# Turning k and q of chunks 2 and 3 on TensorE instead of VectorE and DMA, in a kernel of gated linear attention and a SoLU feed-forward block

## The chip, the core and the metric

The kernel runs on one core of one Trainium2 chip. The core has TensorE (PE in the profile; its weight loads are PEld), VectorE (DVE), ScalarE (ACT), GpSimd (POOL) and SyncE (SP, which here only issues DMAs). Each engine executes its own list of instructions in order and waits on semaphores for the others. The metric is the device time of one execution in microseconds (us); lower is better.

## The reference

Two blocks follow each other. The first is a recurrence over 768 time steps for 4 batches and 8 heads with head dimension 48; the second works on the 3072 resulting rows of 384.

```python
mag = np.sqrt(a_re * a_re + a_im * a_im)
scale = np.minimum(mag, 0.999) / (mag + 1e-06)
a_re_n, a_im_n = (a_re * scale, a_im * scale)
for t in range(S):
    ...
    new_re = ar * S_re - ai * S_im
    new_im = ar * S_im + ai * S_re
    kv = np.einsum('bhd,bhe->bhde', k[:, :, t], v[:, :, t])
    S_re, S_im = (new_re + kv, new_im)
    y[:, :, t] = np.einsum('bhd,bhde->bhe', q[:, :, t], S_re)
...
h = x @ w_in
e = np.exp(h - h_max)
sm = e / (np.sum(e, axis=-1, keepdims=True) + 1e-09)
solu = h * sm
ln = (solu - mu) / np.sqrt(var + 1e-06) * g_ln
return (ln @ w_out).astype(np.float32)
```

The weights w_in (384 x 1024), w_out (1024 x 384) and g_ln come as float64 and are converted on the chip.

## The kernel before

**Tiling.** The 768 steps are cut into 6 stretches of 128, so there are 24 chunks (stretch times batch), numbered c = stretch * 4 + batch. Two chunks make a group g; the gates of a group are prepared together. So group 0 holds chunks 0 and 1, group 1 holds chunks 2 and 3.

**Preparing a group** (prep_steps, L793). From a_re and a_im the magnitudes and angles are formed by a chain that alternates between ScalarE and VectorE: `inverse` (Ln, Exp), `ratio` (two products on VectorE), `sure`, `tangent`, `square`, `secant`, `size`, `eps`, `lnm`. `total0/1` sums the logarithms over time on TensorE (f_L, L848), `grow` and `decay` are four Exp on ScalarE, `trig` loads the table for trigonometric functions, `angle` is an arctangent, `phase0/1` sums the angles on TensorE (f_phase, L848), `nearest` and `part` wrap them, `sin` and `cos` fill the tile f_cs, `exp` (a step of that name) loads the Exp table again. `qs` and `ks` scale q and k. In group 0 the first part runs in two halves, with a or b at the end of the step's name. The steps `last` and `onward` are small DMAs that hand the end of a stretch on.

**Turning k and q** (turn_steps, L949). `k2` and `q2` on VectorE (L957) multiply k and q by cosine and sine into f_kq, 128 x (2, 8, 96). For the scores it is needed with time in the free dimension (f_kqT). There are two ways. Chunks in the list `SHORT_KQ` (0 and 1) go through TensorE: `kt0, kt1, qt0, qt1` each transpose four heads into PSUM (f_turned, L978, four instructions), and `kT0, kT1, qT0, qT1` copy them on ScalarE (L984). The PSUM pool `ps_t` for this has two buffers, which f_L, f_phase, f_tot, f_zt, f_parts and f_count use too. All other chunks go through `kqb`, one transpose of 32 x 32 blocks on VectorE (f_kb, L966), and `kqt0`, four DMAs from SP that put the blocks in place (L971).

**A chunk** (chunk_steps, L998). `score0/1` (TensorE, L1011), `mask0` (VectorE, L1016), `values` (TensorE, L1044, result f_y), and, except in the last stretch, `carry` (TensorE, f_d, L1052) and `add` (VectorE, state).

**The feed-forward part of a chunk** (ffn_steps, L1073). `turned_x` copies f_y to f_xT on ScalarE (L1078); `up0/1` multiply by w_in (f_h, L1085); `exp0` is the exponential on ScalarE with its sum; `solu` the product on VectorE; then z is turned (`zt/zT` through TensorE and ScalarE for the chunks in `SHORT`, `blocks/away` through VectorE and DMA for the others); `down0/1` multiply by w_out (f_o, L1162); `centred`, `spread`, `norm`, `scale` normalise; `store` is the output DMA. In the trace TensorE's float32 matmuls stand as two records each.

**The weights** (weight_steps, L721). Seven pieces, 0 to 2 of w_in and 3 to 6 of w_out, are fetched as float64 into one of three buffers f_raw (`fetch`), and converted: `raised` on ScalarE (L746), `convert` on VectorE in three instructions (L752, L754, L756). `mean` 0 to 7, `meansum` and `centre` 0 to 7 subtract the mean from w_out. Near the end each piece is fetched again (`again`) and looked at for its least magnitude (`inspect`, L759); `judge`, `judges`, `judgew`, `count` and `flag` end in a flag that chooses between ending and a slower general program.

**What sets the order.** Everything is written out by hand: the string ORDER (L515 to L600) names every step with its index, and the loop at L1257 issues them in this order. The order of the instructions of one engine is the order in which the string names its steps; there is no scheduler. SP's list of DMAs follows the same string.

Of the kernel before, what the change touches and what calls it, by code (L numbers as in the profile page):

```python
# [515 lines left out]
load_ara:0 inversea:0 load_aia:0 ratioa:0 surea:0 load_arb:0 tangenta:0 inverseb:0 squarea:0 load_aib:0 secanta:0  # L516
fourtha:0 ratiob:0 sureb:0 sizea:0 fetch:5 epsa:0 tangentb:0 squareb:0 secantb:0 lnma:0 fetch:1 raised:5 load_k:0
sizeb:0 fetch:0 epsb:0 total0:0 convert:5 load_q:0 fourthb:0 raised:1 grow0:0 decay0:0 lnmb:0 total1:0 grow1:0 fetch:2
decay1:0 convert:1 trig:0 anglea:0 angleb:0 ks1:0 phase0:0 phase1:0 load_vr:0 raised:0 convert:0 nearest0:0 nearest1:0
load_ar:1 part0:0 cosa:0 sina:0 qs0:0 qs1:0 load_ai:1 part1:0 ks0:0 sinb:0 fetch:6 cosb:0 q2:0 last:0 exp:0 qt0:0  # L520
qT0:0 raised:2 k2:0 qt1:0 qT1:0 kt0:0 kt1:0 load_v:0 q2:1 convert:2 kT0:0 inverse:1 fetch:3 fetch:4 gain:0 kT1:0 qt1:1
raised:6 k2:1 score0:0 onward:0 kt0:1 qT1:1 score1:0 turn_ends:0 ratio:1 kT0:1 load_k:1 sure:1 mask0:0 tot:0 tangent:1
values:0 convert:6 square:1 turned_x:0 secant:1 fourth:1 qt0:1 raised:3 size:1 convert:3 eps:1 qT0:1 load_q:1 lnm:1
up1:0 up0:0 raised:4 exp0:0 convert:4 total1:1 total0:1 grow1:1 ks1:1 decay0:1 grow0:1 decay1:1 trig:1 kt1:1 load_ar:2
angle:1 carry:1 kT1:1 phase0:1 ks0:1 load_ai:2 qs0:1 last:1 nearest0:1 solu0:0 phase1:1 nearest1:1 part0:1 score1:1
part1:1 score0:1 sin:1 mask0:1 zt1:0 qs1:1 cos:1 add:1 mean:0 load_q:2 mean:1 exp:1 mean:3 zT1:0 q2:2 values:1 k2:2
mean:7 inverse:2 load_v:1 mean:5 mean:4 mean:2 turned_x:1 mean:6 turn_ends:1 kqb:2 ratio:2 meansum:0 carry:0 up0:1
kqt0:2 centre:6 zt0:0 tot:1 sure:2 centred:0 centre:5 tangent:2 centre:7 square:2 up1:1 score0:2 score1:2 secant:2
spread:0 centre:4 centre:1 centre:0 size:2 zT0:0 k2:3 eps:2 centre:2 centre:3 down0:0 load_vr:1 fourth:2 q2:3 lnm:2
total1:2 exp0:1 total0:2 kqb:3 decay0:2 grow1:2 load_k:3 grow0:2 mask0:2 add:0 decay1:2 trig:2 down1:0 load_k:2  # L530
solu0:1 angle:2 on:2 values:2 kqt0:3 onward:1 zt0:1 centred:1 qs0:2 turned_x:2 zT0:1 carry:2 phase1:2 phase0:2 last:2
load_ar:3 nearest0:2 norm:0 score0:3 score1:3 ks1:2 nearest1:2 part0:2 scale:0 part1:2 sin:2 add:2 up1:2 cos:2
load_ai:3 up0:2 mask0:3 ks0:2 exp:2 q2:4 k2:4 inverse:3 values:3 exp0:2 load_v:2 turn_ends:2 load_q:3 zt1:1 kqb:4
ratio:3 zT1:1 solu0:2 turned_x:3 sure:3 down0:1 centred:2 tangent:3 kqt0:4 down1:1 tot:2 spread:1 square:3 zt1:2
secant:3 zt0:2 qs1:2 size:3 up1:3 carry:3 zT0:2 q2:5 k2:5 load_vr:2 fourth:3 eps:3 up0:3 store:0 norm:1 scale:1
score1:4 lnm:3 zT1:2 kqb:5 total1:3 add:3 total0:3 onward:2 exp0:3 load_ar:4 score0:4 down0:2 decay0:3 decay1:3
grow1:3 mask0:4 grow0:3 load_k:4 solu0:3 kqt0:5 qs0:3 centred:3 down1:2 blocks:3 spread:2 trig:3 angle:3 values:4 on:3
turned_x:4 phase1:3 phase0:3 last:3 norm:2 ks0:3 nearest0:3 carry:4 nearest1:3 part0:3 load_v:3 score1:5 ks1:3 away:3
part1:3 score0:5 add:4 up1:4 sin:3 cos:3 scale:2 qs1:3 exp:3 store:1 load_ai:4 spread:3 load_q:4 up0:4 mask0:5
turn_ends:3 inverse:4 q2:6 values:5 k2:6 kqb:6 exp0:4 ratio:4 turned_x:5 solu0:4 sure:4 tangent:4 down0:3 norm:3  # L540
kqt0:6 down1:3 centred:4 square:4 blocks:4 carry:5 secant:4 size:4 up1:5 tot:3 store:2 k2:7 eps:4 q2:7 scale:3 up0:5
score1:6 lnm:4 score0:6 onward:3 kqb:7 exp0:5 away:4 total1:4 load_vr:3 fourth:4 load_ar:5 total0:4 down0:4 decay0:4
solu0:5 grow1:4 grow0:4 mask0:6 decay1:4 trig:4 kqt0:7 centred:5 qs0:4 angle:4 down1:4 blocks:5 add:5 spread:4 on:4
store:3 values:6 away:5 phase0:4 last:4 turned_x:6 phase1:4 norm:4 ks0:4 nearest0:4 carry:6 nearest1:4 part0:4 part1:4
add:6 score0:7 sin:4 score1:7 ks1:4 up1:6 scale:4 up0:6 mask0:7 qs1:4 load_ai:5 turn_ends:4 spread:5 load_q:5 down0:5
cos:4 q2:8 values:7 exp:4 k2:8 inverse:5 kqb:8 exp0:6 ratio:5 load_k:5 down1:5 turned_x:7 solu0:6 sure:5 tangent:5
kqt0:8 carry:7 square:5 blocks:6 secant:5 norm:5 away:6 load_vr:4 fourth:5 up0:7 size:5 up1:7 k2:9 eps:5 q2:9
centred:6 score0:8 tot:4 score1:8 lnm:5 total0:5 kqb:9 scale:5 total1:5 load_v:4 exp0:7 decay0:5 down0:6 grow1:5
grow0:5 mask0:8 decay1:5 solu0:7 kqt0:9 qs0:5 down1:6 add:7 centred:7 spread:6 values:8 blocks:7 trig:5 angle:5
onward:4 on:5 last:5 phase0:5 turned_x:8 norm:6 phase1:5 away:7 ks0:5 nearest0:5 carry:8 nearest1:5 up1:8 part1:5  # L550
part0:5 store:5 scale:6 add:8 score0:9 sin:5 cos:5 score1:9 ks1:5 qs1:5 load_ar:6 load_ai:6 spread:7 load_q:6 up0:8
# [59 lines left out]
def whole(ctx, tc, flag, q, k, v, a_re, a_im, moe_w_in, moe_w_out, moe_g_ln, out):  # L611
# [58 lines left out]
    least = const.tile([P, 7], FP, name="f_least")  # L670
    T, steps = {}, {}

    SHORT_KQ = [0, 1]

    SHORT = [0, 1, 2, 23]

# [642 lines left out]
```

## Time and profile before

| | us |
|---|---|
| median of 3 runs | 423.92 (423.43 to 425.55) |
| the profiled execution, its time | 421.44 |
| its span in the trace | 419.1 |
| DVE busy | 331.8 (79%) |
| ACT busy | 287.5 (69%) |
| DMA queue of SP, share of 16 engines' span | 72.3% |

The profile is of one execution. Its groups of instructions give a count and a mean duration; the costliest on TensorE:

```profile
L1085 PE MATMUL f_h<-f_w_in,f_xT 128*32 128x512 f32 x1152 | 130.7, 593 | 0.4 <-ACT f_xT L1078 0.4
L1162 PE MATMUL f_o<-f_w_out,f_zT 128*32 128x384 f32 (+1 forms) x1344 | 130.1, 486 | 0.3 <-ACT f_zT L1117 0.2
```

The columns are line, engine, operation, output <- inputs, partitions x elements, count | busy us, mean ns of one | idle us of the engine just before them and what ended it. Matmuls overlap, so busy time is less than count times mean. A row of 40 digits gives the busy share of each fortieth of the span (10.5 us) in tenths.

### The profile page before, as it was taken

What the parts mean: (1) busy time and instruction counts of PE and PEld (TensorE: products, weight loads), DVE (VectorE), ACT (ScalarE), POOL (GpSimd) and SP (SyncE); (2) the same over time, 40 slices, a digit from 0 to 9 for tenths busy, and PEclk for the clock granted to TensorE, in tenths of its full rate; (3) what the DMA queues carried; (4) which work ended last, traced back from release to release, by engine and by line L of the source; (5) the groups of instructions that cost most, each with busy time, mean ns of one, the idle gap of its engine ahead of it and who ended that gap; (6) DMA issues with size and microseconds to landing.
All of it is one profiled execution on the core that took longest, in us unless ns stands there. A gap on an engine that the chain in (4) does not pass through costs nothing.

```text
span 419.1 us, 15795 instructions
## 1 busy us (share of the span) xinstructions
PE 381.9 (91%) x6928; PEld 200.4 (48%) x6928; DVE 331.8 (79%) x429; ACT 287.5 (69%) x468; POOL 57.0 (14%) x139
## 2 busy tenths in 40 slices
PE   0258779999999999999999999999999999999993
PEld 0025344555554554554555555555455544545441
DVE  4899899788799689699699599689798798774550
ACT  5898978888577768677667767866866885621440
POOL 3000000321210201021211211102111111010210
PEclk9988999999999999999999999999999999999998
DMA  8999436875858738769589857788868869478970
GB/s 235 311 262 215 86 83 127 180 159 113 194 137 173 176 93 179 151 149 206 122 191 201 176 125 157 189 180 192 167 141 196 167 156 204 94 170 256 328 260 28
DMA packets 167261, 72.58 MB, mean 173 GB/s; under 512 B 142480, under 2 KB 155792, under 8 KB 166416
## 3 DMA queue, kind: packets, MB, share of 16 engines
q1 hardware_dynamic: 167040, 71.17, 72.3%
q8 instruction: 56, 0.92, 0.9%
q10 hardware_dynamic: 144, 0.33, 0.3%
q14 instruction: 21, 0.17, 0.1%
HBM read 38.87 MB, written 4.72 MB: 104 GB/s over the span
## 4 chain that ended last, share of the span: by engine, by line
PE 79%; ACT 9%; DMA 4%; DVE 3%; issue 2%; SPq 0%; POOL 0%; DVEq 0%; ACTq 0%; POOLq 0%
PE f_o L1162 28%; PE f_h L1085 26%; PE f_y L1044 9%; PE f_score L1011 5%; PE f_phase L848 4%; PE f_L L848 4%; PE f_d L1052 3%; DMA f_ar<-in_a_re_dram 2%; DMA f_raw<-in_moe_w_out_dram 1%; DMA f_kqT<-f_kb 1%; PE f_zt L1112 1%; ACT f_cs L912 1%; ACT L946 1%; DVE f_kb L966 1%; ACT f_cs L907 1%
## 5 line engine op out<-in xcount | busy, mean ns | idle before, releaser
L1085 PE MATMUL f_h<-f_w_in,f_xT 128*32 128x512 f32 x1152 | 130.7, 593 | 0.4 <-ACT f_xT L1078 0.4
L1162 PE MATMUL f_o<-f_w_out,f_zT 128*32 128x384 f32 (+1 forms) x1344 | 130.1, 486 | 0.3 <-ACT f_zT L1117 0.2
L1162 PEld LDWEIGHTS f_o<-f_w_out,f_zT 128*32 128x32 f32 (+1 forms) x1344 | 55.0, 114 | 64.9 <-issue 55.0
L1085 PEld LDWEIGHTS f_h<-f_w_in,f_xT 128*32 128x32 f32 x1152 | 39.7, 110 | 64.8 <-issue 64.0
L966 DVE STREAM_TRANSPOSE f_kb<-f_kq 128x1536 f32<-128x1536 f32 x22 | 56.0, 2544 | 2.6 <-DMA f_kqT<-f_kb 2.2
L1095 ACT ACTIVATE f_z<-f_h 128x1024 f32<-128x1024 f32 x24 | 28.6, 1193 | 15.5 <-PE f_h L1085 15.5
L1078 ACT COPY f_xT<-f_y 128x384 f32<-128x384 f32 x24 | 11.4, 474 | 39.8 <-PE f_y L1044 39.8
L1011 PEld LDWEIGHTS f_score<-f_kqT 96*32 96x32 f32 x1536 | 32.7, 111 | 10.4 <-issue 9.8
L1044 PE MATMUL f_y<-f_att,f_v 128*32 128x128 f32 (+1 forms) x384 | 36.1, 273 | 1.2 <-DVE f_att L1016 1.2
L1104 DVE SCALAR_TENSOR_TENSOR f_z<-f_h,f_z 128x1024 f32<-128x1024 f32 (+1 forms) x36 | 33.4, 962 | 3.9 <-ACT f_z L1095 3.9
L1044 PE MATMUL f_y<-f_att,f_vr 128*32 128x128 f32 x384 | 36.4, 273 | 0.0
L1140 POOL TENSOR_SCALAR f_less<-f_sum 128x1 f32<-128x1 f32 x24 | 13.1, 546 | 163.4 <-DVE f_z L1104 152.7
L1016 DVE TENSOR_TENSOR f_att<-f_score,f_mats 128x1024 f32<-128x1024 f32 x24 | 29.1, 1213 | 7.2 <-PE f_score L1011 7.2
L903 DVE SCALAR_TENSOR_TENSOR f_f<-f_f,f_phase 128x384 f32<-128x384 f32 x24 | 13.0, 552 | 26.8 <-ACT f_f L899 26.5
L848 PE MATMUL f_L<-f_lr,f_mats 128*32 128x384 f32 x192 | 19.3, 518 | 15.7 <-DVE f_lr L843 15.7
L1011 PE MATMUL f_score<-f_kqT 96*32 96x32 f32 (+3 forms) x1536 | 32.8, 236 | 0.0
L1044 PE MATMUL f_y<-f_kqT,f_state 96*32 96x128 f32 (+1 forms) x640 | 32.7, 272 | 0.0
L1143 ACT ACTIVATE f_z<-f_z,f_less 128x1024 f32<-128x1024 f32 x24 | 27.5, 1147 | 0.0
L1166 ACT ACTIVATE f_ot<-f_o,f_rs 128x384 f32<-128x384 f32 x24 | 13.7, 573 | 16.5 <-POOL f_rs L1151 6.0
L1044 PEld LDWEIGHTS f_y<-f_att,f_v 128*32 128x32 f32 (+1 forms) x384 | 21.8, 103 | 6.2 <-issue 3.8
L1122 DVE STREAM_TRANSPOSE f_zb<-f_z 128x1024 f32<-128x1024 f32 x20 | 24.8, 1238 | 0.1
L957 DVE TENSOR_TENSOR f_kq<-f_cs,f_q 128x768 f32<-128x768 f32 x24 | 22.9, 952 | 2.2 <-ACT f_cs L912 1.1
(101 smaller groups left out, 585.2 us busy)
## 6 DMA issues: line engine op xcount, KB each, us to landing
f_kqT<-f_kb SPq DMA_DIRECT2D x88, 192.0 KB, 3.4
f_zT<-f_zb SPq DMA_DIRECT2D x80, 128.0 KB, 3.2
f_raw<-in_moe_w_out_dram SPq DMA_DIRECT2D x16, 384.0 KB, 5.1
f_raw<-in_moe_w_in_dram SPq DMA_DIRECT2D x6, 1024.0 KB, 7.7
f_k<-in_k_dram SPq DMA_DIRECT2D x12, 384.0 KB, 5.2
f_q<-in_q_dram SPq DMA_DIRECT2D x12, 384.0 KB, 5.4
f_v<-in_v_dram SPq DMA_DIRECT2D x12, 384.0 KB, 5.0
out_dram<-f_ot SPq DMA_DIRECT2D x24, 192.0 KB, 3.7
```

Source lines behind the costliest of these rows:

```text
L848: nc.tensor.matmul(out=ps[r:r + 32], lhsT=weights[:, r:r + 32], rhs=st[nm][:, i * DM:(i + 1) * DM], start=True, stop=True)
L957: nc.vector.tensor_tensor(out=t, in0=T["cs", g][:, i * H:(i + 1) * H], in1=heads(T[nm, g][:, i]).unsqueeze(2).to_broadcast([P, H, 2, D]), ...
L966: nc.vector.transpose(out=t, in_=T["kq", c].rearrange("p n h (f j) -> p j (n h) f", j=3))
L1011: nc.tensor.matmul(out=scores[r0:r0 + 32, x, r:], lhsT=QK[:, r // 32, x], rhs=QK[:, r // 32:, H + x], start=True, stop=True)
L1016: nc.vector.tensor_tensor(out=st["att"].rearrange("p (i u) t -> p i u t", u=2), in0=scores.rearrange("p (i u) t -> p i u t", u=2), in1=mat ...
L1044: nc.tensor.matmul(**product)
L1085: nc.tensor.matmul(out=st["h"][r:r + 32, half * 512:(half + 1) * 512], lhsT=st["xT"][:, c * P + r:c * P + r + 32], rhs=w_in[:, c, half * 5 ...
L1095: nc.scalar.activation(out=z, in_=h, func=AF.Exp, accum_out=sums[:, n:n + 1])
L1104: nc.vector.scalar_tensor_tensor(out=z, in0=h, scalar=1.0, in1=z, op0=OP.mult, op1=OP.mult, accum_out=st["sum"][:, 2 + i:3 + i])
L1122: nc.vector.transpose(out=st["zb"], in_=st["z"].rearrange("p (c s f) -> p s c f", s=4, f=32))
L1143: nc.scalar.activation(out=st["z"], in_=st["z"], func=AF.Square, bias=st["less"], accum_out=st["sum"][:, 1:2])
L1162: nc.tensor.matmul(out=st["o"][rows], lhsT=zT, rhs=w_out[:, c], start=(c == 0), stop=(c == KF - 1))
```

## The change

`SHORT_KQ` becomes [0, 1, 2, 3]: chunks 2 and 3 lose their steps `kqb` and `kqt0` and get `kt0, kt1, qt0, qt1` and `kT0, kT1, qT0, qT1`. The functions themselves stay as they are. The whole of ORDER is replaced by another string: all steps that both kernels have are named again, in another order from the first line to the last. In the diff its beginning and its end are shown.

```diff
 ORDER = """
-load_ara:0 inversea:0 load_aia:0 ratioa:0 surea:0 load_arb:0 tangenta:0 inverseb:0 squarea:0 load_aib:0 secanta:0
-fourtha:0 ratiob:0 sureb:0 sizea:0 fetch:5 epsa:0 tangentb:0 squareb:0 secantb:0 lnma:0 fetch:1 raised:5 load_k:0
-sizeb:0 fetch:0 epsb:0 total0:0 convert:5 load_q:0 fourthb:0 raised:1 grow0:0 decay0:0 lnmb:0 total1:0 grow1:0 fetch:2
-decay1:0 convert:1 trig:0 anglea:0 angleb:0 ks1:0 phase0:0 phase1:0 load_vr:0 raised:0 convert:0 nearest0:0 nearest1:0
-load_ar:1 part0:0 cosa:0 sina:0 qs0:0 qs1:0 load_ai:1 part1:0 ks0:0 sinb:0 fetch:6 cosb:0 q2:0 last:0 exp:0 qt0:0
-qT0:0 raised:2 k2:0 qt1:0 qT1:0 kt0:0 kt1:0 load_v:0 q2:1 convert:2 kT0:0 inverse:1 fetch:3 fetch:4 gain:0 kT1:0 qt1:1
-raised:6 k2:1 score0:0 onward:0 kt0:1 qT1:1 score1:0 turn_ends:0 ratio:1 kT0:1 load_k:1 sure:1 mask0:0 tot:0 tangent:1
-values:0 convert:6 square:1 turned_x:0 secant:1 fourth:1 qt0:1 raised:3 size:1 convert:3 eps:1 qT0:1 load_q:1 lnm:1
-up1:0 up0:0 raised:4 exp0:0 convert:4 total1:1 total0:1 grow1:1 ks1:1 decay0:1 grow0:1 decay1:1 trig:1 kt1:1 load_ar:2
-angle:1 carry:1 kT1:1 phase0:1 ks0:1 load_ai:2 qs0:1 last:1 nearest0:1 solu0:0 phase1:1 nearest1:1 part0:1 score1:1
-part1:1 score0:1 sin:1 mask0:1 zt1:0 qs1:1 cos:1 add:1 mean:0 load_q:2 mean:1 exp:1 mean:3 zT1:0 q2:2 values:1 k2:2
-mean:7 inverse:2 load_v:1 mean:5 mean:4 mean:2 turned_x:1 mean:6 turn_ends:1 kqb:2 ratio:2 meansum:0 carry:0 up0:1
...
-store:19 values:22 blocks:21 judge:0 turned_x:22 norm:20 scale:20 score0:23 score1:23 inspect:5 up1:22 mask0:23
-away:21 up0:22 down0:21 again:6 again:4 exp0:22 store:18 solu0:22 blocks:22 values:23 down1:21 turned_x:23 centred:22
-inspect:6 inspect:4 spread:22 spread:21 again:2 store:20 up1:23 norm:21 scale:21 norm:22 up0:23 away:22 again:0
-again:1 down0:22 exp0:23 down1:22 inspect:2 judges:0 scale:22 solu0:23 zt0:23 inspect:1 again:3 zt1:23 zT0:23
-inspect:3 inspect:0 centred:23 store:21 zT1:23 down0:23 judgew:0 spread:23 norm:23 down1:23 store:22 count:0 flag:0
-scale:23 store:23
+load_arb:0 inverseb:0 load_aib:0 ratiob:0 load_ara:0 sureb:0 tangentb:0 load_aia:0 inversea:0 squareb:0 fetch:5
+ratioa:0 fourthb:0 secantb:0 load_k:0 sizeb:0 surea:0 tangenta:0 fetch:1 load_vr:1 epsb:0 squarea:0 secanta:0 lnmb:0
+load_q:0 sizea:0 epsa:0 total1:0 grow1:0 raised:5 fourtha:0 lnma:0 fetch:0 decay1:0 total0:0 decay0:0 grow0:0
+convert:5 trig:0 load_ai:1 anglea:0 ks1:0 phase0:0 angleb:0 ks0:0 load_ar:1 raised:1 nearest0:0 phase1:0 fetch:2
+nearest1:0 convert:1 part0:0 qs1:0 sina:0 qs0:0 cosa:0 part1:0 sinb:0 q2:0 qt1:0 cosb:0 k2:0 last:0 kt0:0 raised:0
+k2:1 convert:0 qT1:0 exp:0 kT0:0 qt0:0 kt1:0 qT0:0 q2:1 inverse:1 kT1:0 kt0:1 score0:0 kT0:1 qt1:1 load_vr:0 qT1:1
+score1:0 turn_ends:0 qt0:1 ratio:1 load_v:0 sure:1 mask0:0 tangent:1 raised:2 square:1 convert:2 qT0:1 values:0
+fetch:6 fetch:3 tot:0 secant:1 turned_x:0 kt1:1 up0:0 size:1 kT1:1 raised:6 convert:6 eps:1 up1:0 fetch:4 fourth:1
+raised:3 lnm:1 convert:3 total1:1 total0:1 exp0:0 score1:1 gain:0 onward:0 load_ar:2 grow1:1 decay1:1 grow0:1 decay0:1
+load_k:1 trig:1 score0:1 solu0:0 angle:1 phase0:1 phase1:1 raised:4 nearest0:1 convert:4 nearest1:1 carry:1 part0:1
+zt1:0 part1:1 sin:1 mean:0 mean:1 mask0:1 load_q:1 mean:3 mean:7 add:1 cos:1 load_ai:2 again:0 mean:2 mean:4 ks0:1
+qs0:1 mean:6 mean:5 q2:2 qs1:1 k2:2 exp:1 values:1 meansum:0 zT1:0 inverse:2 qt0:2 qT0:2 kt0:2 centre:5 turned_x:1
+centre:3 ratio:2 sure:2 kt1:2 kT1:2 carry:0 up1:1 last:1 centre:0 centre:1 kT0:2 qt1:2 tangent:2 square:2 centre:7
+q2:3 secant:2 up0:1 qT1:2 onward:1 zt0:0 size:2 centre:6 centre:4 load_v:1 load_q:2 centre:2 eps:2 zT0:0 qt0:3 qT0:3
...
+down0:20 solu0:21 turned_x:22 again:5 kqt0:23 again:3 store:18 up1:22 inspect:5 score0:23 score1:23 mask0:23 up0:22
+values:23 down1:20 last:11 exp0:22 blocks:21 turned_x:23 again:2 centred:21 spread:21 norm:20 solu0:22 norm:21
+store:19 inspect:3 up1:23 up0:23 scale:20 away:21 blocks:22 centred:22 away:22 exp0:23 down0:21 spread:22 down1:21
+solu0:23 again:1 again:6 zt0:23 store:20 inspect:1 norm:22 centred:23 scale:21 down0:22 down1:22 zT0:23 zt1:23
+store:21 judge:0 inspect:6 judges:0 scale:22 spread:23 zT1:23 again:4 store:22 down0:23 inspect:2 norm:23 inspect:4
+down1:23 judgew:0 count:0 scale:23 store:23 flag:0
 """
...
-    SHORT_KQ = [0, 1]
+    SHORT_KQ = [0, 1, 2, 3]
```

On TensorE the new list begins: f_L and f_phase of group 0, 20 transposes (five halves), score0 of chunk 0, four transposes, score1, f_tot, four, f_y of chunk 0, four, f_h of chunk 0, f_L of group 1, the scores of chunk 1, f_phase of group 1, f_d of chunk 1, f_zt, f_parts, f_y of chunk 1, f_mean, 12 transposes of chunk 2, f_d of chunk 0, half of f_h of chunk 1, four transposes, the other half, f_zt, four transposes, the scores of chunk 2, f_L of group 2, half of f_o of chunk 0, eight transposes, its other half, four transposes, f_zt, f_y of chunk 2.

## The prediction

> **What bounds the kernel now.** I read the page's busy line and slices first, then TensorE's busy time by stretch, then the chain of waits through the start, then rows of single instructions.
>
> ```profile
> PE 381.9 (91%) x6928; PEld 200.4 (48%) x6928; DVE 331.8 (79%) x429; ACT 287.5 (69%) x468; POOL 57.0 (14%) x139
> ...
> PE   0258779999999999999999999999999999999993
> ```
>
> TensorE works for 381.9 of 419.1 us, and its digits fall short of 9 only in the first six slices and in the last one. The stretches say it to the tenth:
>
> ```profile
> core 0: us, PE busy (x) PEld busy (x) DVE busy (x) ACT busy (x) POOL busy (x), PEclk, DMA share, GB/s
> 0.00:60.17 60.17, 30.49 (x419) 15.38 (x419) 49.45 (x79) 50.38 (x85) 4.08 (x14) 0.94 0.80 200
> 60.17:75.14 14.97, 14.90 (x201) 7.25 (x204) 14.93 (x24) 11.58 (x18) 0.00 (x0) 1.00 0.69 145
> 75.14:405.20 330.06, 329.85 (x6289) 173.92 (x6289) 263.66 (x322) 222.28 (x360) 51.19 (x119) 1.00 0.75 175
> 405.20:411.90 6.70, 6.46 (x28) 3.82 (x26) 3.48 (x5) 2.72 (x5) 1.74 (x7) 1.00 0.14 54
> 411.90:419.10 7.20, 0.16 (x3) 0.05 (x2) 0.29 (x2) 0.58 (x1) 0.00 (x0) 0.82 0.13 41
> ```
>
> Up to 60.17 us TensorE is idle for 29.7 us (60.17 - 30.49); from there to 411.9 for 0.5 us in all; then come 7.2 us of last scale, store and flag. So the span is 29.7 idle + 381.9 work + about 7.5, and only two things can move it: TensorE work added or removed, and the length of the start. In the start VectorE (49.5) and ScalarE (50.4) are the full engines, each running its list in written order. How the start ends is seen in the chain of waits (start, length, what):
>
> ```profile
> 56.32 0.58 ACT f_zT L1117
> 56.91 0.75 ACT f_lr L808
> 57.68 0.84 ACT f_x L809
> 58.52 0.37 ACT f_xT L1078
> 58.89 0.38 ACT f_meanp L775
> ...
> 59.34 0.89 PE f_mean L777 x2
> 60.24 0.77 PE f_d L1052 x45
> ...
> 61.05 2.57 PE f_h L1085 x23
> ```
>
> ScalarE hands over xT of chunk 1 and the partial means, TensorE does the mean and carry:0, and from f_h of chunk 1 (at 60.87 with its first pipelined matmuls) it is never without work again. That instant is my reference point.
>
> **The prices.**
>
> ```profile
> L978 PE MATMUL f_turned<-f_mats,f_kq x32: 272/421/450, 27.2 to 48.0; 128*96 128x128 f32 x32
> ...
> L984 ACT COPY f_kqT<-f_turned x8: 562/570/592, 28.7 to 50.0; 96x512 f32<-96x512 f32 x8
> ```
> ```profile
> L966 DVE STREAM_TRANSPOSE f_kb<-f_kq x22: 2305/2462/3127, 56.9 to 371.8; 128x1536 f32<-128x1536 f32 x22
> ...
> DMA to landing us min/median/max: 2.6/3.4/5.3
> ```
> ```profile
> 37.87 0.64 PE L978 MATMUL f_turned<-f_mats,f_kq 128*96 128x128 f32 x4
> ```
>
> Single transposes overlap, so their 421 ns is not the price; four of them, one half of k or q, take 0.64 us at full clock, 0.16 each.
>
> *Removed:* two block transposes of chunks 2 and 3 on VectorE (2.31 and 2.32 us there, at 56.90 and 69.63) and their eight DMAs, 2.5 us of SP's issuing per chunk. Worth on the path: nothing. Chunk 2's score starts at 66.7, and between 58 and 80 us no wait of TensorE names f_kqT's DMA; what hides the route is f_h and f_zt of chunks 1 and 0 (61.05 to 66.9). Without that cover it would cost 2.3 + 2.6 (SP) + about 3 us.
>
> *Added:* 32 transposes, 8 x 0.64 = 5.1 us of TensorE, and 8 copies, 8 x 0.57 = 4.6 us of ScalarE. After the reference point every transpose lengthens the span, since nothing there is idle. The written order on TensorE puts 12 of them (three halves of chunk 2) between f_mean and f_d, before f_h of chunk 1, and 20 behind it: 5 x 0.64 = **3.2 us** on the path for certain.
>
> [...]
>
> *Moved:* the order before the reference point. I walk the new lists with durations of the old rows.
> (a) Up to the return to the exp tables at 27.4 us both lists hold the same work (b's half now first); I take no difference, bounds -0.6 to +0.6.
> (b) f_h of chunk 0 starts at 38.86 now, when xT is copied. In the new ScalarE list the copy of xT stands behind sure, raised:2, square, a copy of q, f_tot and secant of group 1. VectorE's ratio ends at 34.9 in both orders, its mask at about 36.2 (36.7 now); from there tangent 0.96, square 0.84, copy 0.57, f_tot 0.15, secant 0.94, xT 0.46 give 40.1 with gaps. The mask can also come up to 1.1 later: the second half of the scores waits for a transpose that waits for a copy behind two 0.85 us instructions on ScalarE, while TensorE's clock stands at 0.50 (27 to 34 us). I take 40.3: **+1.4**, bounds +1.0 and +2.2. The third piece of w_in is converted behind tangent now, 0.69 + 1.22 + 1.23 = 3.1 us, ready at 40.3 to 41.4; only the last third of each half of f_h needs it, so the first 1.7 us of f_h hide it.
> (c) From f_h of chunk 0 to phase of group 1 takes 11.3 us now (38.86 to 50.16): f_h, exp:0, four exps, table load, arctan. The same chain stands in the new list, so 51.6. Then raised:4 (0.95) is ahead of nearest, and convert:4's last step on VectorE waits for it with both part steps queued behind: **+0.3**, bounds 0 and +1. The cosines, done at 55.01 now, come at 56.7 and the exp tables at 58.0 (56.3 now).
> (d) Then ScalarE has meanp 0.48, zT 0.58, Ln 0.75, Exp 0.84, a copy of q 0.57, xT 0.46: 61.7. TensorE has mean (59.5), two halves of chunk 2 (60.7), the third, which waits for one of two PSUM buffers until that copy ends at 61.2, so 61.9, and carry:0 0.65: 62.5. The second decides: f_h of chunk 1 at 62.5 instead of 60.87, **+1.7** in all; the 12 transposes, 1.9 us, lie inside this wait for ScalarE, and without it would be paid in full.
>
> *Queues.* On SP the fetch of the last w_out piece now waits for a raw buffer until about 39 us (30.70 now), and g_ln, onward:0, ar of group 2, k and q of group 1 stand behind it. k issues near 44 and lands within some 5 us (5.2 in the median for f_k, by the table of DMA issues), and ks1:1 comes at 57: cover 8 us, beyond which each us counts. load_v of group 1 now stands behind onward:1 (about 55) and is wanted by values:2 at 80. The early again:0 fetch adds 1 MB near 46 us, where DMA moves 5 GB/s now (45 to 50 us). All at nothing.
> *Behind the reference point:* ScalarE's seven further copies stand between table loads and spread:0, and TensorE waits for them through the two PSUM buffers; I walked to values:2 and found waits of at most 0.3 each: 0, bounds 0 and +2. In the end stretch down:21 (5.16) now covers exp and solu of chunk 23 (5.0) where down:22 did, and count still follows down:23: 0, bounds -0.3 and +1. The last inspected fetch (again:4) lands some 3 us ahead of count.
>
> **Sum:** +1.7 + 3.2 = +4.9, less 0.1 for gaps of now that close: +4.8. The profiled execution took 421.44 us (span 419.1 and 2.3 around it), so its like would take 426.2; the median of the runs is 423.92, 2.5 above the profiled one, so I forecast 423.92 + 4.8 = **428.7**. Terms at their low ends: 1.0 - 0.6 + 3.2 - 0.3 = +3.3; at their high ends: 2.2 + 0.6 + 1 + 3.2 + 2 + 1 = +10.0, which will not come together.
>
> **Rivals.**
> R1, not slower: *the start shortens.* ScalarE is idle for 5.54 us between 4.70 and 58.43 (53.73 less 48.19 busy). If the new order closed all of that, xT would end at 58.9 + 1.05 (meanp and a copy, ahead of it now) - 5.54 = 54.4 and f_h of chunk 1 start at 55.05: -5.8 + 3.2 = -2.6, 421.3. It decides where f_h of chunk 1 starts before 57.7 (60.87 - 3.2); in the middle, 56.4, the time is 422.6. For: the order is new throughout, and I can't exclude that idle closes. Against: the walk finds f_h of chunk 0 later, and VectorE too is 82% full up to 60 us.
> R2: *ScalarE holds the transposes up.* The copy of one half of chunk 3 follows spread:0 (1.35) and a table load (1.28), that of a half of chunk 2 follows an instruction that waits for VectorE's ratio:2 (about 1.3). If TensorE has nothing queued ahead of them, +3.9: 432.6. For: two buffers, one list in order. Against: f_h and f_o of 2.6 us stand between on TensorE.
> R3: *a stall further on,* from the new order of 75 to 405 us: now 0.2 us in 330. One late kqT chain (block 2.5, issue 2.5, landing 3.4) with a cover short by 2 us gives 430.7. Nothing points at a place.
>
> **How the numbers follow.** Forecast 0.70 (its own range 426.5 to 431), R1 0.13, R2 0.10, R3 0.07. A change under 0.5%, 2.1 us, can't be told from none here: faster is under 421.8, slower over 426.0. R1 gives 0.06 faster and 0.06 same; the forecast's low edge 0.03 same; the rest is slower: 0.06, 0.09, 0.85. The range reaches from the upper half of R1 (425.6) to R2 (432.6).
>
> **What would show it.** TensorE's busy time up by 5 us (382 to 387), VectorE's block transposes 20 instead of 22, L984 x16; f_h of chunk 0 near 40.3 and of chunk 1 near 62.5; no more than 1 us idle on TensorE from there to the last f_o. Wrong if f_h of chunk 1 comes before 58, if eight halves cost well under 5 us of TensorE, or if idle of several us shows behind 75 us.

## The result and the profile after

The changed kernel takes 427.56 us in the median of 7 runs (426.67 to 428.24), the kernel before 422.85 in the median of its 7 runs beside them (420.99 to 425.55). The ratio is 1.0110, with a 95% interval of 1.0076 to 1.0145: 4.7 us slower. The forecast was 428.7 with a range of 425.6 to 432.6. It stood on 423.92 for the kernel before, the median of three runs; that median is 422.85 with seven, so it is the +4.8 of the forecast that compares with +4.7, and 428.7 was 1.1 too high.

The profiled execution took 426.8 us, its span is 424.6 (before: 421.44 and 419.1). First the page of the changed kernel, busy line and TensorE's digits:

```profile
PE 388.6 (92%) x6960; PEld 217.3 (51%) x6960; DVE 328.3 (77%) x427; ACT 291.2 (69%) x476; POOL 56.8 (13%) x139
...
PE   0367689999999999999999999999999999999993
```

TensorE has 6.7 us more work, VectorE 3.5 less, ScalarE 3.7 more. The same engine in stretches, cut where f_h of chunk 1 starts and where the end begins:

```profile
core 0: us, PE busy (x) PEld busy (x) DVE busy (x) ACT busy (x) POOL busy (x), PEclk, DMA share, GB/s
0.00:62.31 62.31, 33.75 (x469) 18.09 (x472) 48.58 (x79) 50.97 (x85) 5.20 (x15) 0.97 0.86 217
62.31:75.00 12.69, 12.69 (x172) 5.97 (x163) 11.02 (x21) 11.65 (x20) 0.00 (x0) 1.00 0.55 104
75.00:80.00 5.00, 4.49 (x24) 3.08 (x24) 2.22 (x4) 4.54 (x7) 1.62 (x6) 1.00 0.46 91
80.00:410.50 330.50, 330.42 (x6283) 186.53 (x6285) 264.34 (x321) 221.21 (x360) 48.97 (x115) 1.00 0.71 165
410.50:424.60 14.10, 7.20 (x38) 3.64 (x30) 2.09 (x6) 2.85 (x5) 1.04 (x3) 0.95 0.21 76
```

From 62.31 us on TensorE is idle only for 0.5 us near 79, 0.3 ahead of the last f_o, and in the last scale and store. The picture is the old one, with a later start and more work behind it. Last TensorE's timeline (start, length, what; in brackets the idle time ahead and what ended it):

```profile
39.54 5.36 PE L1085 MATMUL f_h<-f_w_in,f_xT 128*32 128x512 f32 x48 [0.63 <-ACT f_xT L1078]
...
50.82 2.53 PE L848 MATMUL f_phase<-f_x,f_mats 128*32 128x384 f32 x16 [3.51 <-ACT f_x L886]
...
58.53 0.91 PE L777 MATMUL f_mean<-f_meanp,f_mats 128*128 128x384 f32 x2 [1.02 <-ACT f_meanp L775]
59.28 1.05 PE L978 MATMUL f_turned<-f_mats,f_kq 128*96 128x128 f32 x8
61.10 0.64 PE L978 MATMUL f_turned<-f_mats,f_kq 128*96 128x128 f32 x4 [0.78 <-ACT f_kqT L984]
...
62.38 2.75 PE L1085 MATMUL f_h<-f_w_in,f_xT 128*32 128x512 f32 x23
65.06 0.64 PE L978 MATMUL f_turned<-f_mats,f_kq 128*96 128x128 f32 x4
65.63 2.78 PE L1085 MATMUL f_h<-f_w_in,f_xT 128*32 128x512 f32 x24
...
75.02 1.08 PE L978 MATMUL f_turned<-f_mats,f_kq 128*96 128x128 f32 x8
75.93 2.75 PE L1162 MATMUL f_o<-f_w_out,f_zT 128*128 128x384 f32 x8
78.51 0.60 PE L978 MATMUL f_turned<-f_mats,f_kq 128*96 128x128 f32 x4
79.62 0.66 PE L1112 MATMUL f_zt<-f_mats,f_z 128*128 128x128 f32 x4 [0.51 <-ACT f_kqT L984]
```

Read the start of one row to the start of the next: that is what a row costs on the path. Four transposes move f_h from 65.06 to 65.63 (0.57), another four the scores from 68.84 to 69.37 (0.53), eight move f_o from 75.02 to 75.93 (0.91), the last four end at 79.11 (0.60). Together 2.61 us, and behind them stands a wait of 0.51 for a copy of ScalarE.

So the 5.5 us of span divide as follows. The start: 62.38 against 60.87, +1.5, which is one execution against one. From there to f_count, the last of TensorE (417.76 and 411.86 us): 355.38 against 350.99, +4.4, of which 2.6 are transposes, 0.5 the wait, and 1.3 lie in no single place. Behind f_count: 6.84 against 7.24, -0.4. The 1.3 is of the size by which executions of one list differ: the kernel before with unread matmuls in its start, below, has the same instructions behind f_h of chunk 1 and needs 352.32 for them, 1.3 more as well.

### The profile page after: what moved, and what is told of

It reads as the page before. It is cut to its first block, busy times and chain, and to the rows that moved or that the text cites. A ratio compares the mean times of both kernels' runs of the same rounds, so it can differ in the third digit from the quotient of the medians.

```text
span 424.6 us, 15860 instructions
## 1 busy us (share of the span) xinstructions
PE 388.6 (92%) x6960; PEld 217.3 (51%) x6960; DVE 328.3 (77%) x427; ACT 291.2 (69%) x476; POOL 56.8 (13%) x139
## 4 chain that ended last, share of the span: by engine, by line
PE 83%; ACT 10%; DVE 3%; issue 1%; DMA 1%; ACTq 0%; DVEq 0%
PE f_o L1162 28%; PE f_h L1085 28%; PE f_y L1044 9%; PE f_score L1011 6%; PE f_phase L848 4%; PE f_L L848 3%; PE f_d L1052 3%; DMA f_ar<-in_a_re_dram 1%; ACT L943 1%; ACT f_kqT L984 1%; PE f_turned L978 1%; ACT f_z L1095 1%; ACT f_u L829 1%; ACT f_ar L826 1%; ACT f_u L839 1%
## 5 line engine op out<-in xcount | busy, mean ns | idle before, releaser
L1162 PEld LDWEIGHTS f_o<-f_w_out,f_zT 128*32 128x32 f32 (+1 forms) x1344 | 60.5, 114 | 60.2 <-issue 47.1
L1085 PEld LDWEIGHTS f_h<-f_w_in,f_xT 128*32 128x32 f32 x1152 | 46.2, 110 | 61.6 <-issue 56.4
L966 DVE STREAM_TRANSPOSE f_kb<-f_kq 128x1536 f32<-128x1536 f32 x20 | 50.2, 2508 | 2.3 <-DMA f_kqT<-f_kb 1.8
L1095 ACT ACTIVATE f_z<-f_h 128x1024 f32<-128x1024 f32 x24 | 29.3, 1221 | 28.7 <-PE f_h L1085 28.4
L1011 PE MATMUL f_score<-f_kqT 96*32 96x32 f32 (+3 forms) x1536 | 34.6, 236 | 0.0
L1044 PE MATMUL f_y<-f_kqT,f_state 96*32 96x128 f32 (+1 forms) x640 | 34.4, 272 | 0.0
L848 PE MATMUL f_L<-f_lr,f_mats 128*32 128x384 f32 x192 | 20.5, 517 | 14.3 <-DVE f_lr L843 14.3
L1149 POOL TENSOR_SCALAR f_s<-f_s,f_sum 128x1 f32<-128x1 f32 x24 | 10.5, 439 | 140.8 <-ACT f_z L1143 140.2
L1143 ACT ACTIVATE f_z<-f_z,f_less 128x1024 f32<-128x1024 f32 x24 | 27.4, 1142 | 0.0
L848 PE MATMUL f_phase<-f_x,f_mats 128*32 128x384 f32 x192 | 20.4, 540 | 6.4 <-ACT f_x L886 6.4
L1044 PEld LDWEIGHTS f_y<-f_att,f_vr 128*32 128x32 f32 x384 | 23.6, 109 | 2.4 <-issue 2.1
```

Source lines behind the costliest of these rows:

```text
L848: nc.tensor.matmul(out=ps[r:r + 32], lhsT=weights[:, r:r + 32], rhs=st[nm][:, i * DM:(i + 1) * DM], start=True, stop=True)
L966: nc.vector.transpose(out=t, in_=T["kq", c].rearrange("p n h (f j) -> p j (n h) f", j=3))
L1011: nc.tensor.matmul(out=scores[r0:r0 + 32, x, r:], lhsT=QK[:, r // 32, x], rhs=QK[:, r // 32:, H + x], start=True, stop=True)
L1044: nc.tensor.matmul(**product)
L1085: nc.tensor.matmul(out=st["h"][r:r + 32, half * 512:(half + 1) * 512], lhsT=st["xT"][:, c * P + r:c * P + r + 32], rhs=w_in[:, c, half * 5 ...
L1095: nc.scalar.activation(out=z, in_=h, func=AF.Exp, accum_out=sums[:, n:n + 1])
```

## The experiments

Every kernel was timed beside the kernel before on its chip; the median of before moved between 422.9 and 424.0 from one set of runs to the next, on one chip between 423.1 and 424.0, so the ratios are what to compare. "us" is the ratio less one, times 423.

| run | median | ratio (95%) | us |
|---|---|---|---|
| changed kernel | 427.56 | 1.0110 (1.0076 to 1.0145) | +4.7 |
| new order, old route | 430.24 | 1.0159 (1.0133 to 1.0185) | +6.7 |
| old order, new route | 434.68 | 1.0258 (1.0210 to 1.0307) | +10.9 |
| new order, chunk 2 alone by TensorE | 426.87 | 1.0079 (1.0055 to 1.0103) | +3.3 |
| the same, a fetch issued later | 426.54 | 1.0059 (1.0031 to 1.0087) | +2.5 |
| changed, transposes twice | 429.48 | 1.0150 (1.0125 to 1.0176) | +6.3 |
| before, 20 unread transposes | 425.45 | 1.0057 (1.0027 to 1.0088) | +2.4 |
| changed, f_d earlier | 427.08 | 1.0100 (1.0052 to 1.0149) | +4.2 |
| changed, f_d earlier and twice | 427.53 | 1.0086 (1.0056 to 1.0116) | +3.6 |
| changed, f_d earlier and four times | 427.23 | 1.0111 (1.0062 to 1.0161) | +4.7 |
| before, unread matmuls in the start | 422.39 | 0.9979 (0.9945 to 1.0013) | -0.9 |
| changed, the same and f_d twice | 427.70 | 1.0089 (1.0055 to 1.0123) | +3.8 |

### What a transpose costs

**Each transpose twice.** In the changed kernel:

```diff
-            for j in range(4):
+            for j in list(range(4)) * (2 if c in (2, 3) else 1):
                 nc.tensor.transpose(out=ps[0:D2, j], in_=T["kq", c]...
```

> The changed kernel with each transpose of chunks 2 and 3 issued twice into the same place: nothing left out, 32 transposes more on TensorE and no copy more. Theory: the 20 behind f_h of chunk 1 cost 20 x 0.16 = +3.2 again; the 12 ahead of it lie in the wait for ScalarE's xT but the third group starts only at 61.10 and gets 0.64 longer, f_d and f_h of chunk 1 so 0.3 to 0.7 later: +3.2 to +4.0, 430.8 to 431.6. [...] Rival (transposes lie beside other work): under +1.

429.48 against 427.56: +1.9 (+1.7 by the ratios), below the +3.2 to +4.0 expected, above the "under +1" of transposes that lie beside other work. Its timeline says why:

```profile
62.81 2.75 PE L1085 MATMUL f_h<-f_w_in,f_xT 128*32 128x512 f32 x23
65.49 1.08 PE L978 MATMUL f_turned<-f_mats,f_kq 128*96 128x128 f32 x8
66.50 2.78 PE L1085 MATMUL f_h<-f_w_in,f_xT 128*32 128x512 f32 x24
...
76.29 1.95 PE L978 MATMUL f_turned<-f_mats,f_kq 128*96 128x128 f32 x16
78.08 2.75 PE L1162 MATMUL f_o<-f_w_out,f_zT 128*128 128x384 f32 x8
```

Eight now take 1.01 from start to start where four took 0.57, sixteen 1.79 where eight took 0.91. Four more cost 0.44, that is 0.11 per transpose; a group on its own pays some 0.1 for changing over. Along the path: f_h of chunk 1 0.43 later, then 0.44, 0.44 and 0.88, and -0.24 for the last group, whose second half fills the wait of 0.51: 1.95, where the medians say 1.9. The two profiled executions are 2.7 apart; the other 0.7 lie behind 81 us, where the lists are the same. And f_h of chunk 0 came 0.31 earlier here under the same list, so that the 12 further transposes of the start cost more than the 0.43. My expected 0.64 per group was the length of a record, and records overlap at both ends.

**20 transposes that nothing reads, in the kernel before.** A new step, put behind up0:1, zt0:0, down0:0 and down1:0 in the old order:

```diff
+    def dead(n):
+        for _ in range(n):
+            ps = ps_t.tile([P, 4, P], FP, tag="t", name="f_dead")
+            for j in range(4):
+                nc.tensor.transpose(out=ps[0:D2, j], in_=T["kq", 2][:, 0, j], identity=ident)
```

> The kernel before with 20 transposes more on TensorE (f_dead, into PSUM, read by nothing), in groups of 4, 4, 8 and 4 behind f_h of chunk 1, where the changed kernel has its 20; route, order and copies stay as before, nothing is left out. In the trace of the changed kernel a group of four moves the next start by 0.53 to 0.57 and one of eight by 0.91, and in the run with doubled transposes four more in the same place cost 0.44. Theory (TensorE is full behind f_h of chunk 1, so its work is paid there whatever the order): 0.55 + 0.55 + 0.91 + 0.55 = +2.6, 425.3 to 426 beside a median of 423.1 of before. By the prediction's price (0.64 a group) +3.2. Rival (the old order has slack that takes them in): under +1.

425.45 beside 423.06, +2.4 by the ratio (1.1 to 3.7), where 2.6 was expected. The profiled execution was a long one (432.1, with stretches at half rate up to 63 us), so only steps are read from its timeline:

```profile
68.84 0.64 PE L1252 MATMUL f_dead<-f_mats,f_kq 128*96 128x128 f32 x4
69.32 0.60 PE L1112 MATMUL f_zt<-f_mats,f_z 128*128 128x128 f32 x4
69.76 0.60 PE L1252 MATMUL f_dead<-f_mats,f_kq 128*96 128x128 f32 x4
70.29 2.78 PE L1085 MATMUL f_h<-f_w_in,f_xT 128*32 128x512 f32 x24
...
76.81 1.04 PE L1252 MATMUL f_dead<-f_mats,f_kq 128*96 128x128 f32 x8
77.78 1.50 PE L848 MATMUL f_L<-f_lr,f_mats 128*32 128x384 f32 x16
```

Steps of 0.48, 0.53 and 0.97, close to the 0.53 to 0.57 and 0.91 of the changed kernel. The old order has no slack for them: TensorE's share of the route, 2.4 to 2.6 us, is paid in either order.

### The order without the route, the route without the order

**New order, old route.** ORDER of the changed kernel, less the sixteen turn and copy steps of chunks 2 and 3:

```diff
-    SHORT_KQ = [0, 1, 2, 3]
+    SHORT_KQ = [0, 1]
 ...
+ k2:2 kqb:2 ... load_q:2 kqt0:2 ... k2:3 kqb:3 ... load_q:4 kqt0:3
```

> The changed kernel's written order with the old route back for chunks 2 and 3 (VectorE's block transposes behind k2 and their DMAs): nothing is computed differently. Theory (the 32 transposes are what costs): the 20 behind f_h of chunk 1 go (-3.2), the 0.5 us wait at 79.6 goes, and f_h of chunk 1 comes 0 to 1 us earlier than 62.3, since xT still waits for ScalarE's chain; TensorE's busy time falls by 5 us. 422.5 to 424.5, 3.2 to 4.7 under the changed kernel and within 1 us of the kernel before. Rival (the new order costs, not the route): stays at 426.5 to 428. Third way (the blocks on VectorE now delay another thing): above 425 with idle of TensorE behind 62 us.

430.24: slower than the changed kernel, not faster. My theory missed by 6 us, and the rival with 426.5 to 428 too; the third way came closest. The timeline, VectorE first:

```profile
59.67 2.28 DVE L965 STREAM_TRANSPOSE f_kb<-f_kq 128x1536 f32<-128x1536 f32 x1
...
71.70 0.96 DVE L842 SCALAR_TENSOR_TENSOR f_lr<-f_lr,f_u 128x768 f32<-128x768 f32 x1
```
```profile
61.96 6.82 PE L1084 MATMUL f_h<-f_w_in,f_xT 128*32 128x512 f32 x47
...
72.81 1.50 PE L847 MATMUL f_L<-f_lr,f_mats 128*32 128x384 f32 x16 [1.86 <-DVE f_lr L842]
...
83.58 0.77 PE L1010 MATMUL f_score<-f_kqT 96*32 96x128 f32 x32 [1.68 <-issue]
```

Between 56 and 78 us VectorE is busy for 21.2 of 22 us. A block transpose of 2.28 in this list makes everything behind it 2.3 later: f_lr of group 2 starts at 71.70 instead of 69.44, and TensorE waits 1.86 for it. The scores of chunk 3 come 1.68 late, by the times for their DMAs (the block transpose ended at 76.4, the DMAs were issued until 79.0 and land within 5.1), though the profile names no releaser. And f_h of chunk 1 takes 6.82 for 47 where 5.3 is usual: in place of the 12 transposes TensorE stood idle for 1.56, and its clock fell (0.74 from 61.6 to 68.0 us). Idle of 1.9, 1.7 and 0.4, and 1.5 of half rate, are more than the 2.6 + 0.5 that went.

**Old order, new route.** ORDER of before, where the steps of chunks 2 and 3 take the places of kqb and kqt0 (tot:1 moves ahead of them):

```diff
+ meansum:0 tot:1 qt0:2 kt0:2 qT0:2 kT0:2 carry:0 up0:1 qt1:2 kt1:2 qT1:2 kT1:2
 ...
+ down1:0 qt0:3 kt0:3 ... on:2 qT0:3 kT0:3 values:2 qt1:3 kt1:3 qT1:3 kT1:3
```

> The old written order with the new route alone: the transposes of chunks 2 and 3 stand where their block transposes and DMAs were used, 8 of them behind f_mean and ahead of f_h of chunk 1, the others behind it; nothing is computed differently. Theory: 24 transposes behind the reference point or on its path, 24 x 0.16 = +3.8, the first 8 ahead of carry:0 and f_h of chunk 1 up to +1.3 more, waits for ScalarE's copies 0 to +1: 427 to 429 against 422.9 of the kernel before, f_h of chunk 1 at 61 to 62.3. Rival (the order is the cost): 422.5 to 424.

434.68 (431.14 to 437.04), beyond both. Timeline of ScalarE, VectorE, TensorE:

```profile
68.15 1.07 ACT L984 COPY f_kqT<-f_turned 96x512 f32<-96x512 f32 x2 [3.33 <-PE f_turned L978]
69.11 0.94 ACT L818 ACTIVATE f_u<-f_x,f_bias 128x768 f32<-128x768 f32 x1
```
```profile
70.17 0.96 DVE L823 SCALAR_TENSOR_TENSOR f_x<-f_x,f_ai 128x768 f32<-128x768 f32 x1 [5.57 <-ACT f_u L818]
```
```profile
76.16 2.82 PE L1162 MATMUL f_o<-f_w_out,f_zT 128*128 128x384 f32 x8 [2.88 <-DVE f_w_out L780]
```

The copies of the second halves stand on ScalarE ahead of f_u, the next link of the gates of group 2. They wait 3.33 for transposes that stand on TensorE behind half of f_h; VectorE waits 5.57 for f_u, with the centring of w_out queued behind, and TensorE waits 2.88 for that. This execution also lost 3.05 up to f_mean, where the lists are still the same: its f_h of chunk 0 took 6.89 instead of 5.36, with matmuls of 1.06 us up to 43.6 us and of 0.59 from there on, which is half rate and full. So up to 3 us of its time are not the route's.

So the four corners are 0 (old, old), +6.7 (new order), +10.9 (new route, where I had put it) and +4.7 (both). The parts don't add: the new order is fitted to the new route.

**Chunk 2 alone by TensorE.** The changed kernel with `SHORT_KQ = [0, 1, 2]`, kqb:3 behind k2:3 and kqt0:3 behind load_q:4:

> The changed kernel with chunk 3 alone back on the old route (block transpose and DMAs); chunk 2 keeps its transposes; nothing is computed differently. Theory: the 16 transposes of chunk 3 all stand behind f_h of chunk 1, where TensorE is never idle: 4 x 0.64 = -2.6, and -0.5 for the wait at 79.6, which is on a copy of chunk 3: 424.4 to 425.1, f_h of chunk 1 at 62.3 as in the changed kernel. Rival (transposes cost little, the start's order all): 427 to 428. Rival (chunk 2 costs as much as chunk 3): this run halves the difference to the blocks-again kernel.

426.87, +3.3 by the ratio: 1.3 under the changed kernel where 2.5 to 3.1 was expected, and with intervals that overlap not shown to be better at all. In its trace f_phase of group 2 starts at 78.62 instead of 81.11; 2.1 of that was gained from f_h of chunk 1 on, the rest before it, where the lists are the same. Then it gives 2.74 back in one place, and 1.15 in another (f_zt at 406.92, for VectorE's product, a wait that the changed kernel doesn't have). The chain of waits (start, length, what), and the DMA queue of kind instruction in the window 389 to 390 (packets, MB, share):

```profile
388.12 1.16 PE f_y L1044 x41
389.28 2.74 issue
392.02 0.75 PE f_y L1044 x17
```
```profile
q8 instruction: 1, 0.02, 5.5%
```

TensorE stops in the midst of f_y, between two matmuls of the same kind, and waits for nothing that the profile shows.

**The same with a fetch issued later:**

```diff
- turned_x:23 again:2 centred:21
+ turned_x:23 centred:21 ... centred:22 away:22 again:2
```

> The run with chunk 3 alone on the old route, with one 1 MB fetch of the closing check (again:2, f_raw from w_in) issued some 16 us later on SP; nothing is left out. In that run TensorE stood still for 2.74 us in the midst of f_y (389.3 to 392.0) without a wait, with one 16 KB packet of the queue of kind instruction in that stretch, and so it ended only 1.3 under the changed kernel although it led by 2.5 at 80 us. Theory (TensorE ran out of instructions because their fetch lay behind the loaded DMA engines): with the megabyte gone from 382 to 389 the standstill shrinks below 1 us and the time is 424 to 425.5. Rival (the standstill hangs on the place in the list alone): it stays at 2 to 3 us, 426 to 427. Rival (the later fetch is late for its check): idle ahead of f_count at the end.

In the profiled execution (424.37) no standstill is left, and from f_h of chunk 1 to f_count it takes 354.0 against 357.0. But the runs lie between 424.2 and 429.1, median 426.54, +2.5: not apart from the run without the edit. This trace is of one of its fastest runs, the one with the standstill of the slowest of six, so the two show extremes. The standstill went in the execution that was looked at; that the moved megabyte was its cause is not shown.

### The clock in the start

In the changed kernel TensorE is idle for 3.51 us ahead of f_phase, which then takes 2.53 instead of 1.50. The granted clock (the third number from the end) in three of its microseconds:

```profile
51.00:52.00 1.00, 1.00 (x12) 0.39 (x8) 0.39 (x1) 0.58 (x1) 0.36 (x2) 0.57 1.32 230
52.00:53.00 1.00, 1.00 (x12) 0.25 (x7) 0.84 (x2) 0.58 (x1) 0.00 (x0) 0.50 1.47 235
...
54.00:55.00 1.00, 1.00 (x28) 0.85 (x22) 0.99 (x3) 0.79 (x2) 0.00 (x0) 0.72 1.08 426
```

I had foreseen none of this. Three runs move f_d of chunk 1 into the pause, once, twice or four times:

```diff
- nearest1:1 carry:1 part0:1
+ score0:1 carry:1 solu0:0 ...
-            for x in range(H):
+            for x in list(range(H)) * (2 if c == 1 else 1):
```

> The changed kernel with one step moved on TensorE: f_d of chunk 1 goes ahead of f_phase of group 1, into the 3.51 us idle between 47.3 and 50.8, which becomes about 2.7; nothing is left out. Theory (the clock falls to 0.50 from 51 to 54.3 because TensorE was idle for 3.5 us; pauses of 1.9 did not do it): either the shorter pause keeps the clock, then f_phase takes 1.50 instead of 2.53, f_h of chunk 1 comes 0.6 to 1.0 earlier and the time is 426.6 to 427; or 2.7 us is still too long (the trace of before has the clock falling after 3.26), then only 0.3 to 0.9 is gained, by f_d's place alone. Rival (the clock falls there for another reason): same clock row, same time.

> The changed kernel with f_d of chunk 1 ahead of f_phase of group 1 and issued twice into the same place (work is repeated, none left out), so that TensorE's pause before f_phase is about 1.9 instead of 3.51 (2.84 in the run with f_d once, where the clock fell all the same; 2.25 in the run with f_d four times, where it held). Theory (the pause lets the clock down, and the half rate costs f_phase and what follows 1.0): from the start of f_h of chunk 0 to that of f_h of chunk 1 takes 21.8 to 22.2 instead of 22.77 in the changed kernel and 22.96 with f_d once; 426.3 to 426.9. Rival (ScalarE sets this stretch): 22.7 or more, 427.5.

> As the run with f_d of chunk 1 ahead of f_phase, with these matmuls issued four times into the same place, so that TensorE pauses for 0.1 to 0.6 us there instead of 3.5; work is only repeated. Theory: the clock stays at 1.00 from 47 to 56, f_phase takes 1.50 instead of 2.53, the phases, cosines and exp tables come 1.0 earlier, f_h of chunk 1 at 61.2 to 61.7 instead of 62.31: 426.4 to 427.0, 0.6 to 1.1 under the changed kernel. Rival (ScalarE and VectorE set the start, f_phase's second half is not on their path): clock held, but f_h of chunk 1 at 62.2 and the time unchanged.

Once: pause 2.84, f_phase 2.73, from f_h of chunk 0 to that of chunk 1 22.96 (changed kernel 22.77): the clock fell all the same. Twice: pause 2.14, f_phase 1.85, 22.07, the expected time, though the clock fell 1 us into f_phase. That the shorter pause did it isn't shown: the changed kernel's own list of the start took 22.00 and 22.94 in the two runs with chunk 2 alone. Four times the clock held, but f_d ran into f_phase:

```profile
46.09 2.73 PE L1052 MATMUL f_d<-f_v,f_kq 128*32 128x48 f32 x180
51.07 0.37 PE L1052 MATMUL f_d<-f_v,f_kq 128*32 128x48 f32 x12 [2.25 <-issue]
51.26 1.48 PE L848 MATMUL f_phase<-f_x,f_mats 128*32 128x384 f32 x16
```

Again a standstill of 2.25 without a wait, in the midst of equal matmuls. From f_phase to f_mean takes 6.68 here and 7.71 in the changed kernel: the half rate costs 1.0 there. All three ratios lie inside the changed kernel's interval: no gain in time is shown.

**The clock held from the beginning.** Unread matmuls on constants in TensorE's first pauses, in the kernel before and, with f_d twice, in the changed one:

```diff
+    def keep(n):
+        ps = ps_y.tile([P, DM], FP, tag="y", padded_shape=[P, 512], name="f_keep")
+        for _ in range(n):
+            for r in range(0, P, 32):
+                nc.tensor.matmul(out=ps[r:r + 32], lhsT=tri[:, r:r + 32], rhs=mats[:, 0:3], start=True, stop=True)
```

> The kernel before with matmuls on constants that nothing reads (f_keep, 16 ahead of f_L of group 0, 12 in each of the next three pauses of TensorE, 2.6 to 3.3 us long), so that the clock is not let down between 0 and 27 us; otherwise as before, nothing left out. In before f_phase of group 0 takes 2.79 instead of 1.50 and the transposes and scores of chunk 0 run at half rate from 27 to 34 us. Theory (these slow stretches lie on the path to f_h of chunk 0, but beside ScalarE's and VectorE's chains for most of it): f_phase 1.3 earlier, of which ScalarE's waits for it (0.16 and 0.70) can be gained, and up to 0.6 at the mask: f_h of chunk 0 0.5 to 1.5 earlier, 421.5 to 422.6 beside 423.1. Rival (start set by VectorE and ScalarE alone, clock without weight): 423 +- 0.4. Rival (the extra matmuls run into the real ones): above 423.5.

> The changed kernel with the unread matmuls on constants in TensorE's first pauses, as in the kernel before with them (422.4), and with f_d of chunk 1 twice ahead of f_phase; work is only added. The clock should then be held in both, so the two differ by the change without its clock effects. Theory: 20 transposes 2.5, the wait behind them 0.5, order 0 to 1: f_h of chunk 1 at 59.8 to 60.5, 425.4 to 426.5, 3.0 to 4.1 above the kernel before with such matmuls and 1 to 2 under the changed kernel. Rival (the clock was the cost of the change): within 1 us of 422.4. Rival (the extra matmuls bring a standstill as in the run with f_d four times): 427 or more.

In the kernel before f_phase of group 0 then takes 1.50 instead of 2.79, eight transposes 1.05 instead of 1.75, and f_h of chunk 0 starts at 38.02 instead of 38.86, 0.84 earlier, as expected; the time is 422.39, ratio 0.9979 with 1 inside its interval. It is the only version here that may beat both kernels, and it isn't shown to. The changed kernel with the same comes to 427.70, and its f_h of chunk 1 starts at 62.13, not at 59.8 to 60.5: in that execution the clock fell at 26.5 and at 50.4 all the same (0.56 from 50 to 53.5), the second time behind a pause of 1.39:

```profile
50.38 2.78 PE L848 MATMUL f_phase<-f_x,f_mats 128*32 128x384 f32 x16 [1.39 <-ACT f_x L886]
```

So the length of the last pause doesn't decide alone: behind 1.39 the clock fell here, behind 1.63 with 1.08 and behind 1.88 in the kernel before it did not. The traces of the two kernels, cut from the first of their clock changes on into stretches of 3.41 us, the shortest time between two changes in them, have TensorE busy for 0.18 ahead of one fall (23.95 to 27.36, before) and for 0.32 ahead of the other (47.73 to 51.14, changed), and up to 80 us for 1.72 or more in each stretch at full rate behind which the rate stayed full. Here TensorE was busy for 1.41 from 47 to 50, and the clock fell at 50.4; with f_d four times it was busy for 2.82 from 46 to 49 and idle from 49 to 51, and the row stands at 1.00 from 46 to 56. What decides, these few cases don't show.

What was meant as a comparison of both kernels without clock effects is none, then, and its gap (3.8 and -0.9) says nothing of the clock. But at most the 1.5 of the start can be the clock's: from 54.6 us in the changed kernel and from 34.2 in the kernel before the rate is full up to the end of TensorE's work, and 3.1 of the change, transposes and wait, lie there.

## Why the prediction was right, and where its steps were off

**The bound** held: TensorE is almost never short of work from f_h of chunk 1 on (0.5 us near 79, 0.3 ahead of the last f_o), and what is added behind it is paid. Shown by the unread transposes (+2.4) and the doubled ones (+1.9, step by step).

**Removed, "worth nothing on the path"**: true for chunk 3, whose block transpose came back without a wait of f_L (in the run with chunk 2 alone), and wrong for chunk 2 in the new order, where the block transpose, put behind k2:2, costs TensorE 1.86. I costed the removal against the old order's cover alone. The sum isn't touched by it, since it was made along the new lists.

**The 20 transposes**, +3.2, measured 2.61. The mis-sized step is 0.64 per group, a record's length; start to start a group is 0.53 to 0.60, a double one 0.91, so that eight groups come to some 4.3 and not to 5.1. A single record is 273 ns here in the median (the 421 of before is that at a granted clock of 0.50, 27.4 to 34.2 us), but records overlap, and the runs show 0.11 us for one transpose more in a group and 0.13 to 0.14 in a group of four.

**The waits behind, "0, bounds 0 and +2"**: 0.51, the second rival's mechanism at an eighth of its price of 3.9. ScalarE's copy of a half of chunk 3 does come behind spread:0 and a table load, and f_o covers most of it. 2.61 and 0.51 make 3.12, close to the 3.2 by luck. The whole is luck in part too: the traces add up to 1.5 + 2.6 + 0.5 + 1.3 - 0.4 = 5.5, the medians differ by 4.7, and the forecast was 1.7 + 3.2 - 0.1 = 4.8.

**The start.** (a) The exp tables come back at 27.80 against 27.40, within the bounds. (b) f_h of chunk 0 at 39.54, +0.7 instead of +1.4, below its low bound of +1.0. Both executions come to full rate at 34.1 to 34.2 us, so like stands beside like. The walk was too long in two places: the mask ended at 36.01 instead of 36.2 or later (`ratio` ended at 33.77, not at 34.9), and the six steps from there to the end of xT took 3.47, where the prediction added up 3.92 of records that overlap. (c) f_phase follows 11.28 behind it (11.30 before), as walked. The +0.3 for raised:4 did not come, since `nearest` waits for f_phase anyway (0.54); in its place f_phase at half rate cost 1.0, which no step had. The cosines, walked to 56.7, ended at 56.69, by two errors that cancel. (d) f_h of chunk 1 at 62.31 against 62.5: +1.5 instead of +1.7. The 12 transposes lay inside the wait for ScalarE for the most part: without them the same order starts f_h at 61.84, 0.5 earlier, but at half rate. All of this is one execution against one: the changed kernel's start, unchanged in the two runs with chunk 2 alone, reached f_h of chunk 1 at 61.94 and 61.42 too, and the old one at 66.09 in the run with unread transposes.

**The rivals.** R1 needed f_h of chunk 1 before 57.7; it came at 62.31. (The prediction calls its lower bound of 425.6 the upper half of R1, but R1 ends where nothing is gained, at 423.9.) R3 needed a stall behind 80 us; there are 0.08 us of idle in 330. R2 came in small.

Open: 1.3 of the 4.4 behind the reference point has no place, and is as large as the difference between executions of one list. The start's 1.5 has not been divided by an experiment between order, transposes and clock.

## What to carry to other kernels

TensorE, full to the end here, turned added instructions into time (20 unread transposes, +2.4); price an instruction from start to start in the trace, not by the length of its record. Before a route is moved from one engine to another, look which engine is full where the instruction stands: in this order the route saves 1.9 us of waits for chunk 2, where VectorE has no pause, and for chunk 3 no wait that it saves was seen. A written order and a route belong together: swapped alone they cost 6.7 and 10.9 us, together 4.7 (with some of the 10.9 the clock's), because each engine here ran its list in written order: a block transpose of 2.28 on VectorE made f_lr 2.3 later, and copies that waited 3.33 on ScalarE held up f_u.

## What the hardware showed beyond that

**Half-rate stretches of 3.4 and 6.8 us.** Worked out from the shares of the clock row, the rate is halved in the changed kernel from 51.1 to 54.6, in the run with f_d earlier from 49.9 to 53.3, with the unread matmuls from 50.4 to 53.8, and in the kernel before from 27.4 to 34.2: 3.4 us or twice that. The row doesn't show all of it: in the changed kernel eight transposes near 30 us took 1.94, as in the kernel before at 0.50, under a row of 1.00. The trace's list of clock changes begins there only at 34.1 us, with the first full rate, and the row counts what lies ahead of that as 1.00; but a transpose's record is 420 ns ahead of it and 273 behind. This first entry lies at 24.0 us in the kernel before and at 43.6 in the run with the old order and the new route, whose lists on TensorE are the same up to f_mean; there its 3.05 went, 1.65 up to f_h of chunk 0 and 1.53 in it. In eight executions of the changed kernel's start it lies between 23.1 and 38.7, and f_h of chunk 0 starts between 38.48 and 39.94: at 38.5 in the three with full rate from 29.3 to 29.5 on, at 39.5 or 39.7 with 34.1 or 34.2, at 39.8 or 39.9 with 38.5 or 38.7.

**Standstills of TensorE without a wait.** 2.74 and 2.25 us between equal matmuls, in two runs whose lists on TensorE differ in length from the changed kernel's, each with one packet of the instruction queue (16 KB each: 0.93 MB in 57) near its beginning (389 to 390, and 48 to 49 us); with f_d twice there is one of 1.3 and, with the unread matmuls, one of 0.6, both without such a packet inside; the kernels before and after have none. One packet comes every 7.5 us, so that a stretch of 2.5 us holds one in a third of cases by chance. The runs show that the two longest stand with a packet, not more.
